# Local attention and a rational-gated MLP in one kernel: one pair of score tiles in other PSUM banks, and the first 259 places of the list of all engines in another order

## The chip, the cores and the metric

The kernel runs on one core of a Trainium2 chip. The metric is device microseconds of one execution, the median of several. A profile of one further execution, with its own time, stands beside the times.

## The reference

Attention over 4 batches, 8 heads, 768 positions, head size 64: each query sees the keys less than 16 positions away, and 24 block keys (the maximum over 32 keys each) whose values are the means of 32 values. Then an MLP with 2048 hidden units over the 3072 tokens of 512 numbers.

```python
k_sum = k.reshape(B, H, nb, 32, D).max(axis=3)
v_sum = v.reshape(B, H, nb, 32, D).mean(axis=3)
scores_l = scale * q @ k.T          # kept where |i - j| < 16
scores_s = scale * q @ k_sum.T + log(32)
a = softmax(concat[scores_l, scores_s])
x = a @ concat[v, v_sum]            # -> (3072, 512)
h = x @ w_in
P = a0 + a1*h + a2*h**2 + a3*h**3
Q = 1 + |b0|*|h| + |b1|*h**2
out = (P / (Q + 1e-06)) @ w_out
```

## The kernel before

The attention is cut into 48 halves of 64 queries (12 to a batch, all 8 heads at once). The MLP is cut into 6 groups of 512 tokens, a group being 8 halves, times 16 chunks of 128 hidden units. Chunk n (n = 0 to 95) is first-layer product, gate and second-layer product; a group's first chunk needs the x of all 8 halves of that group, so no MLP product can start before the first 8 halves are through.

All work is written out by hand as one list, `ORDER` (lines 68 to 113, 1698 places). A wrapper around each engine (`Kept`) makes every instruction follow the engine's last one, so each engine, and SyncE which issues most loads, works strictly in the order of the list. The letters:

- `K0` to `K3` load the keys of the first batch, one pair of heads each, into `kres`; `d0` to `d3` take the block maxima of one pair on VectorE (`ks`). `Q0` loads the queries of halves 0 and 1, `Q1` those of halves 2 to 7. `S`, `I`, `B`, `c`, `F` load or make constants (`F`: the averaging matrix `avg`, kept in `kres`, and values `vf`).
- `b0` to `b3` are the scores of the pairs of halves (0, 1), (3, 6), (4, 2) and (5, 7) on TensorE, into two PSUM tiles `sc` each. `SCP` says from which pool of banks they come: `o` (four banks, later the second layer's output) or `a` (two banks, later squares of h).
- `a0` to `a7` are the nine steps of such a half: peak on VectorE; exponentials on ScalarE; reciprocal on VectorE; multiplication of `ss` on GpSimd (for halves 3 and 5 on VectorE); transposes on TensorE (`pt`); a copy of them (`pts`); values on TensorE (`av`); `xh` on ScalarE or VectorE; `xl` on VectorE. The exponentials read the score tile, so its bank is free when they are done.
- `V` loads the values of a half, `v` (TensorE) and `m` (copies) make the means of the value blocks; `n` and `o` do that for the second batch.
- `W` loads a weight chunk (w_in and w_out, 1 MB, packed; raw tile `wr`, in four buffers in turn, so that W5 takes the buffer of chunk 1 and W8 that of chunk 4), and `w` are the steps that unpack it on ScalarE, GpSimd and VectorE, for some chunks with a DMA issued by GpSimd that writes or adds (`w<-wr`, `wearly<-wr`).
- `A` loads queries and keys of a later half, `L` and `D` do the block maxima of batch 1, `k` copies block keys.
- `h` is a first-layer product (12 matmuls of 512 columns), `g` and `q` are its gate on ScalarE, VectorE and GpSimd (which makes `gl`), `P` is a second-layer product (12 matmuls) that reads `gh` and `gl` of a chunk; it runs three chunks behind `h`.

The buffer of each tile is also written out by hand, in `SLOTS`. Some places have unused matmuls ahead of them (`FILL`), which do no needed work.

Of the kernel before, what the change touches and what calls it, by code (L numbers as in the profile page):

```python
# [76 lines left out]
P11 g9 g9 g10 w12 M g9 g10 w12 q10 h11 a12 a13 b7 a13 g10 q10 P12 a14 V13 a15 h12 g10 a12 a14 g10 g11 w13 a13 a15 q11 w13 g11 q11 g11 w13 a13 W14 g10
g12 a15 w14 g11 P13 a12 g11 g12 a13 a13 g12 g11 q12 h13 w14 a12 P14 V12 a14 a12 a13 g13 w14 a12 w14 g13 a15 V15 q12 w14 w15 a12 g12 a15 A17 w14 a15
a14 h14 g12 a12 g12 g13 q13 q13 a14 V14 a14 a15 w15 g14 g13 w15 w15 a14 g13 w15 w15 P15 h15 a15 a15 g13 P16 q14 L23 q14 a14 g14 g15 A16 a14 q15 g14
h16 L22 g15 b8 q15 g14 g14 a17 g15 g15 g14 g15 g15 g16 h17 g16 P17 q16 P18 q16 g17 A19 g16 a16 g17 q17 A18 f0 g16 f0 g17 q17 h18 g16 D22 g17 h19 g16  # L80
a17 f0 f0 L21 g18 b9 g17 g17 a16 q18 g18 g18 q18 P19 a17 a19 g18 g18 g18 a16 g19 g19 a19 g19 P20 h20 A21 q19 D21 V16 a17 q19 g19 a17 a16 P21 L20 g20
h21 g20 A20 a19 q20 a16 q20 g19 g19 a18 g20 g20 a16 g21 a18 h22 g20 g21 P22 g20 b10 q21 D20 A22 P23 g22 a20 q21 q22 g21 a18 a19 g21 h23 a19 g22 q22
g21 g22 g22 a20 g21 g23 h24 g22 V17 a21 g23 q23 a17 q23 g22 g24 P24 A23 g24 P25 g23 q24 g23 q24 a18 h25 z8 g23 a21 g23 g24 z8 b11 a18 A25 g24 g24 a20
g24 g25 a19 g25 h26 a22 P26 z8 a21 g25 q25 A24 P27 z8 V19 a20 V18 a22 J20 q25 g25 h27 a18 a20 g25 g26 g26 q26 q26 a22 a21 a21 g25 D23 a22 a22 g26 g26
g27 z9 g26 P28 a23 q27 z9 k25 z9 k24 z9 g26 a23 h28 a23 g27 J22 g28 V20 a23 g27 q27 P29 h29 g28 b12 a20 g28 V21 q28 g27 g27 q28 g27 a21 z10 a25 a23
g29 V23 z10 g28 a22 g29 z10 g28 P30 g29 z10 q29 a25 g28 q29 a25 g29 h30 A27 g29 g30 h31 g30 V22 a23 q30 a24 q30 P31 g30 g30 g29 g31 a25 g31 g30 q31
z11 g30 q31 A26 z11 b13 P32 z11 g31 U22 g31 z11 g31 a25 a24 h32 h33 P33 a27 g31 P34 g32 g33 g32 q32 q32 g33 q33 g32 U20 g33 f1 f1 g32 g32 q33 h34 g32
a27 g33 A29 J23 g34 g34 g33 f1 q34 g34 g33 f1 h35 q34 g35 g34 g35 A28 g34 P35 h36 q35 q35 g34 P36 a27 h37 g35 g36 g35 a27 a24 g36 q36 g35 g36 g35 q36
J21 h38 a27 g37 a24 a26 U21 b14 q37 g37 g36 g37 P37 g36 P38 a29 L32 g36 g38 A31 a29 q37 g37 g37 a25 g38 U23 q38 g37 a29 h39 g38 a29 q38 g39 g38 g39
g38 P39 h40 L31 a24 a26 g39 q39 a26 V24 q39 g38 g39 g40 P40 g40 g39 g40 q40 g39 h41 g41 q40 a29 g40 g40 q41 q41 g41 A30 g40 h42 D31 P41 a28 P42 g42  # L90
g41 q42 a26 h43 a24 g42 q42 g41 b15 g42 V25 z12 g41 a31 a28 g42 a27 g41 V27 g43 g42 a26 a30 z12 P43 V26 g43 z12 a28 q43 a31 A32 g43 P44 z12 a28 a30
L33 q43 h44 g42 g44 D32 L30 g43 a31 a28 a26 g43 g43 g44 h45 q44 a31 A33 a30 g44 g45 P45 q44 z13 a31 z13 g44 a30 z13 V28 g45 b16 a32 a32 a28 h46 z13
# [684 lines left out]
```

## Time and profile before

| what | us |
|---|---|
| median of 3 runs | 631.63 |
| lowest and highest | 631.36, 637.08 |
| the profiled execution | 630.29 |
| its span, first to last instruction | 628.4 |
| TensorE busy | 615.1 (98%) |
| VectorE busy | 556.5 (89%) |
| ScalarE busy | 453.4 (72%) |
| GpSimd busy | 251.2 (40%) |

The profiled execution is 1.34 us shorter than the median, and 1.9 us longer than its span. TensorE's share is an average; a busy TensorE may still wait within a group of matmuls or run at the lower clock, so its stages are to be looked at one by one.

### The profile page before, as it was taken

How to read it: one execution, taken by the hardware profiler on the slowest of the kernel's cores; microseconds unless marked ns; L12 is line 12 of the kernel's file. 1: busy time of each engine (PE TensorE's matmuls, PEld its weight loads, DVE VectorE, ACT ScalarE, POOL GpSimd, SP SyncE). 2: the span in 40 equal slices, each digit the busy share in tenths (PEclk: the TensorE clock that was granted, in tenths of full speed). 3: DMA queues.
4: the chain of work that ended last, by engine and by line, in shares of the span. 5: the costliest groups of instructions: out<-in, count | busy, mean ns of one | idle time of the engine just before them, and what ended most of it. 6: DMA issues, size and time to landing. Idle time of an engine off the chain costs nothing.

```text
span 628.4 us, 12096 instructions
## 1 busy us (share of the span) xinstructions
PE 615.1 (98%) x4204; PEld 491.8 (78%) x4204; DVE 556.5 (89%) x1068; ACT 453.4 (72%) x1007; POOL 251.2 (40%) x351
## 2 busy tenths in 40 slices
PE   8899989999999999999999999999999999999997
PEld 4577767778888888878888888888888887878885
DVE  4999999999999898899887999999798897867895
ACT  3998989777968677867785777858777675846553
POOL 0974664771424622334353133354143532221231
PEclk9799999999999999999999999999999999999999
DMA  8998799313342740423353433434413122100001
GB/s 331 340 310 329 221 263 284 118 32 103 121 148 83 213 126 18 159 86 119 111 164 101 143 92 113 145 101 134 136 55 105 59 65 74 68 0 2 0 1 67
DMA packets 52180, 80.78 MB, mean 129 GB/s; under 512 B 6472, under 2 KB 33000, under 8 KB 50200
## 3 DMA queue, kind: packets, MB, share of 16 engines
q1 hardware_dynamic: 50328, 74.87, 36.6%
q0 software_dynamic: 1424, 4.92, 3.5%
q8 instruction: 33, 0.54, 0.4%
q10 hardware_dynamic: 368, 0.22, 0.1%
q14 instruction: 27, 0.22, 0.1%
HBM read 60.33 MB, written 14.75 MB: 119 GB/s over the span
## 4 chain that ended last, share of the span: by engine, by line
PE 79%; DVE 9%; ACT 4%; DMA 3%; POOL 2%; issue 1%; SPq 0%; POOLq 0%; DVEq 0%; ACTq 0%
PE po L162 35%; PE h L162 35%; PE sc L162 4%; PE av L162 4%; DVE tu L162 3%; DVE tq L162 2%; ACT ta L162 2%; DMA w<-wr 1%; PE pt L162 1%; DVE gh L162 1%; DMA kres<-in_kraw_dram 1%; POOL gl L162 1%; DVE wr L162 1%; DMA kr<-in_kraw_dram 1%; DVE sm L162 1%
## 5 line engine op out<-in xcount | busy, mean ns | idle before, releaser
L162 POOL TENSOR_TENSOR gl<-tu,ta 128x512 fp32r<-128x512 f32 x95 | 129.0, 1359 | 325.5 <-DVE tu L162 235.0
L162 PE MATMUL po<-w,gh 128*128 128x512 f32 x384 | 119.9, 394 | 0.0
L162 PE MATMUL po<-wearly,gh 128*128 128x512 f32 x384 | 119.6, 393 | 0.0
L162 PE MATMUL h<-xh,w 128*128 128x512 f32 x384 | 97.8, 393 | 1.7 <-DMA w<-wr 1.5
L162 PE MATMUL h<-xh,wearly 128*128 128x512 f32 x384 | 97.0, 392 | 0.6 <-ACT xh L162 0.6
L162 POOL TENSOR_SCALAR ss<-ss,sm 128x120 f32<-128x120 f32 x184 | 85.8, 487 | 17.1 <-DVE sm L162 9.2
L162 ACT ACTIVATE ta<-tq,cs 128x512 f32<-128x512 f32 x96 | 69.3, 722 | 31.8 <-DVE tq L162 30.2
L162 DVE SCALAR_TENSOR_TENSOR gh<-tu,cs,ta 128x512 fp32r<-128x512 f32 x96 | 77.1, 805 | 11.4 <-ACT ta L162 7.3
L162 PEld LDWEIGHTS h<-xh,w 128*128 128x128 f32 x384 | 71.0, 188 | 18.8 <-DMA w<-wr 2.0
L162 PEld LDWEIGHTS h<-xh,wearly 128*128 128x128 f32 x384 | 71.3, 188 | 16.8 <-ACT xh L162 0.7
L162 ACT ACTIVATE ta<-h,cs 128x512 f32<-128x512 f32 x95 | 64.7, 681 | 26.1 <-POOL gl L162 25.6
L162 PEld LDWEIGHTS po<-wearly,gh 128*128 128x128 f32 x384 | 71.2, 188 | 15.7 <-issue 1.1
L162 PEld LDWEIGHTS po<-w,gh 128*128 128x128 f32 x384 | 71.0, 188 | 15.0 <-issue 0.3
L162 ACT ACTIVATE sq<-h 128x512 f32<-128x512 f32 x72 | 42.0, 583 | 52.5 <-PE h L162 31.6
L162 DVE SCALAR_TENSOR_TENSOR tu<-tu,cs,tq 128x512 f32<-128x512 f32 x96 | 74.9, 780 | 3.4
L162 PE MATMUL po<-wearly,gl 128*128 128x512 f32 x192 | 75.1, 391 | 1.2 <-POOL gl L162 1.2
L162 PE MATMUL po<-w,gl 128*128 128x512 f32 x192 | 75.1, 391 | 0.0
L162 ACT ACTIVATE tu<-h,cs 128x512 f32<-128x512 f32 x96 | 74.5, 776 | 0.0
L162 DVE SCALAR_TENSOR_TENSOR tu<-tu,cs,h 128x512 f32<-128x512 f32 x96 | 71.0, 742 | 1.5
L162 DVE TENSOR_TENSOR tu<-tu,h 128x512 f32<-128x512 f32 x96 | 65.1, 678 | 7.8 <-ACT tu L162 6.6
L162 DVE SCALAR_TENSOR_TENSOR tq<-tq,gh 128x512 f32<-128x512 f32 x96 | 68.6, 714 | 1.8
L162 DVE SCALAR_TENSOR_TENSOR tq<-sq,cs,ta 128x512 f32<-128x512 f32 x72 | 53.4, 743 | 13.7 <-ACT ta L162 13.6
(105 smaller groups left out, 914.1 us busy)
## 6 DMA issues: line engine op xcount, KB each, us to landing
...
cross<-tb SPq DMA_DIRECT2D x32, 256.0 KB
...
out_dram<-o SPq DMA_DIRECT2D x23, 256.0 KB
...
```

Source lines behind the costliest of these rows:

```text
L162: out = getattr(self.engine, name)(*args, **kw)
```

## The change

The first 259 places of `ORDER` hold the same 259 entries in another order; places 260 to 1698 are as before. The third letter of `SCP` becomes `a`, so the score tiles of halves 4 and 2 (`b2`) lie in the two `a` banks. The four score products come as b0, b2, b1, b3 where they came as b0, b2, b3, b1. `SLOTS` is written anew: with it, halves 3 and 6 (`b1`) get the two `o` banks that no tile had before them, and halves 5 and 7 (`b3`) still get those of halves 0 and 1; of all tiles first used after place 259 only two copies (`pts10`, `pts11`) take over from another tile than before, up to a renaming of buffers.

```diff
-SCP = 'ooooaaaa'
+SCP = 'ooaoaaaa'
...
 ORDER = """
-K1 Q0 K0 K3 S K2 W0 w0 d3 d0 w0 d1 d2 b0 a1 a0 Q1 a1 w0 W1 a1 a0 w0 a1 w1 B I b2 a4 b3 a0 a2 a4 W2 w1 a0 a2 w0 a7 F w1 c a4 V7 V4 a1 V3 b1 a2 w2 V6 w0
-w1 a5 V5 a1 w2 w1 a2 a4 V0 w2 a7 w1 a0 v4 v5 v6 a7 k9 a5 v0 a6 V2 a7 v3 V1 A9 v8 v2 A8 a6 w2 v7 a0 v1 v9 m0 a3 a2 W3 a3 a0 w2 a5 a5 W5 m4 a4 m2 a6 m5
-a2 k8 m3 a6 a0 b4 W4 a0 a4 a3 m1 a5 a5 a3 a9 w3 a1 a3 a1 a8 a5 a6 a3 a3 a7 a8 m6 a1 a6 w3 a7 G a2 w3 V8 a5 a2 a3 a8 w5 a4 a6 m7 w2 a7 a6 a6 a5 a2 a4
-w5 a3 a7 w3 w4 a9 w3 a7 a4 a8 h0 V9 w5 g0 w4 w4 L11 h1 w3 a9 w5 n4 n3 g0 W6 q0 g0 w4 q0 W7 g1 w5 n0 w5 g0 A10 n1 a9 a8 a9 a8 a9 g1 g1 g0 q1 q1 g0 g1
-g1 A11 h2 g2 W9 a9 g2 w4 q2 w4 W8 n2 n5 o P3 a9 g2 w6 q2 g1 a9 g2 h3 w6 g3 D11 a8 w6 w7 g2 w7 w6 g3 a8 g2 w6 w9 h4 P4 L10 q3 a8 w7 V11 g4 b5 P5 q3 a10
-q4 g4 g3 g3 g3 w8 w6 h5 q4 w9 a11 w7 g4 w8 h6 g3 A12 a10 g5 P6 w8 g4 g4 g5 q5 w9 w8 g4 w7 w7 L13 W10 a11 q5 a11 P7 g5 w10 D10 w8 g5 V10 a10 h7 w10 g5
...
+K1 K3 d3 d1 K0 S K2 d0 d2 Q0 W0 Q1 b0 b2 w0 a1 a0 b1 a1 a0 w0 w0 W1 a1 V3 V0 a0 w0 b3 w0 a1 k8 a2 w1 w1 a2 a4 k9 I a4 a6 a2 W2 w1 B a6 w2 V2 a0 a2 F
+v3 a4 c a0 V5 V4 V1 a2 V7 v0 a5 V6 v9 a5 a7 a0 w2 a1 v4 v5 v7 a6 w0 v2 a4 w2 a5 w1 a7 v8 a1 v6 a3 v1 w1 m0 a6 w2 a2 A8 m6 a5 w2 w1 a3 A9 a4 m5 W3 W4
+W5 a4 a6 a0 b4 a7 a5 a6 m1 G V8 m2 a5 a6 a0 m4 a3 a8 a3 a7 a6 m7 m3 a2 a3 a2 a3 a1 w3 w3 a6 a5 a0 a9 a2 a7 a8 a3 a7 a3 a5 a4 w3 a4 a5 a8 a1 a7 a4 a3
+a1 a7 w4 w3 a7 w4 h0 w5 w2 h1 w4 a9 n3 w5 n4 w3 n0 w3 w5 a9 a8 n2 g0 n5 w5 n1 g0 W7 W6 q0 q0 V9 g0 w4 w5 w5 a8 a8 g1 h2 w4 a9 g0 g0 L11 g1 a9 o a9 q1
+g0 g1 a8 q1 g1 g2 P3 g1 h3 w4 w6 A10 w7 q2 w6 g2 g2 q2 w7 w6 D11 w6 a9 a8 W9 g2 A11 g2 h4 a8 a9 g1 g3 V11 w6 g2 a9 w6 P4 b5 q3 g3 g4 w7 P5 q3 W8 w9 g3
+q4 a10 h5 g4 L10 g3 g3 q4 w8 w9 a11 w7 g4 w8 h6 g3 A12 a10 g5 P6 w8 g4 g4 g5 q5 w9 w8 g4 w7 w7 L13 W10 a11 q5 a11 P7 g5 w10 D10 w8 g5 V10 a10 h7 w10
...
```

Place 260 is the `w9` of `w9 a11 w7 g4` in the sixth line of either text.

## Rows read from the trace of the kernel before

**Rows 1.** Busy us by stage: length, PE, PEld, DVE, ACT, POOL, clock, DMA share, GB/s.

```profile
5.30:18.95 13.65, 11.16 (x216) 6.41 (x216) 9.98 (x20) 6.82 (x21) 4.29 (x8) 1.00 1.02 398
18.95:25.77 6.82, 5.67 (x73) 3.51 (x73) 6.58 (x14) 6.73 (x28) 6.47 (x8) 0.50 1.07 280
25.77:40.06 14.29, 13.68 (x276) 10.64 (x274) 13.57 (x33) 13.03 (x48) 13.35 (x23) 1.00 1.04 379
40.06:71.55 31.49, 31.07 (x230) 23.88 (x231) 31.07 (x46) 28.99 (x52) 15.98 (x18) 1.00 0.84 271
```

**Rows 2.** TensorE in order of time, 40 to 112 us: start, duration, [idle].

```profile
40.06 2.14 PE L162 MATMUL h<-xh,wearly 128*128 128x512 f32 x8 [0.60 <-ACT xh L162]
...
53.05 0.50 PE L162 MATMUL po<-wearly,gl 128*128 128x512 f32 x1 [0.42 <-POOL gl L162]
...
90.73 1.19 PE L162 MATMUL h<-xh,w 128*128 128x512 f32 x4 [1.55 <-DMA w<-wr]
```

**Rows 3.** GpSimd in order of time, 60 to 92 us.

```profile
75.71 1.29 POOL L162 TENSOR_TENSOR gl<-tu,ta 128x512 fp32r<-128x512 f32 x1 [1.46 <-DVE tu L162]
...
81.38 0.87 POOL L162 DMA_DIRECT2D w<-wr  x1
```

**Rows 4.** Weight loads of TensorE in order of time, 10 to 14 us.

```profile
10.64 0.21 PEld L162 LDWEIGHTS sc<-ks,qres 64*64 64x64 f32 x8 [0.44 <-DVE ks L162]
...
11.49 0.21 PEld L162 LDWEIGHTS sc<-ks,qres 64*64 64x64 f32 x8 [0.53 <-DVE ks L162]
...
13.32 0.21 PEld L162 LDWEIGHTS sc<-kres,qres 64*64 64x64 f32 x8 [0.58 <-DMA qres<-in_qfirst_dram]
```

**Rows 5.** VectorE in order of time, 0 to 36 us.

```profile
7.91 3.53 DVE L162 TENSOR_REDUCE ks<-kres 128x24 f32<-128x768 f32 x4 [6.50 <-DMA kres<-in_kraw_dram]
12.18 0.67 DVE L162 TENSOR_REDUCE sc<-sc 128x4 f32<-128x480 f32 x1 [0.74 <-PE sc L162]
...
20.39 0.28 DVE L162 TENSOR_TENSOR cs<-cs 128x1 f32<-128x1 f32 x1
...
20.89 0.98 DVE L162 TENSOR_TENSOR cs<-cs 128x1 f32<-128x1 f32 x1
...
25.10 1.22 DVE L162 TENSOR_TENSOR wearly<-wr,wearly 128x1024 fp32r<-128x1024 f32 x1
```

**Rows 6.** DMA issues by tile: KB of each.

```profile
kres<-in_kraw_dram SPq DMA_DIRECT2D x4, 400.0 KB
...
qres<-in_qfirst_dram SPq DMA_DIRECT2D x1, 256.0 KB
```

**Rows 7.** ScalarE in order of time, 10 to 46 us.

```profile
11.42 1.16 ACT L162 ACTIVATE wr<-wr 128x1024 f32<-128x1024 f32 x1 [9.39 <-DMA wr<-in_wio_dram]
13.14 0.36 ACT L162 ACTIVATE ss<-sc,sm 128x120 f32<-128x120 f32 x1 [0.56 <-DVE sm L162]
```

**Rows 8.** TensorE in order of time, 8 to 24 us.

```profile
9.71 0.40 PE L162 MATMUL sc<-kres,qres 64*64 64x96 f32 x8
...
15.09 0.40 PE L162 MATMUL sc<-kres,qres 64*64 64x96 f32 x8
...
19.05 0.56 PE L162 MATMUL sc<-bias,hot 96*128 96x480 bf16 x1 [1.66 <-ACT ss L162]
20.66 0.56 PE L162 MATMUL sc<-bias,hot 96*128 96x480 bf16 x1 [1.05 <-ACT ss L162]
21.15 0.60 PE L162 MATMUL sc<-kres,qres 64*64 64x96 f32 x8
```

**Rows 9.** Busy time by stage, columns as in the first group.

```profile
12.18:71.41 59.23, 55.15 (x715) 41.32 (x713) 57.53 (x106) 54.67 (x146) 39.25 (x54) 0.94 0.94 313
...
45.60:71.41 25.81, 25.39 (x208) 19.43 (x206) 25.39 (x38) 23.34 (x38) 13.13 (x13) 1.00 0.85 286
```

**Rows 10.** Busy time of ScalarE alone by stage.

```profile
11.42:43.59 32.17, 30.08 (x105) 0.89 1.04 347
```

**Rows 11.** GpSimd on tile ss, 14 to 48 us: ns least/median/most.

```profile
L162 POOL TENSOR_SCALAR ss<-ss,sm x32: 362/368/2434, 15.6 to 47.2; 128x120 f32<-128x120 f32 x32
```

More of the change, by code (lines that the diff above doesn't have):

```diff
@@ L77 @@
[L77 to L92, printed above, removed]
@@ new lines @@
+g10 g12 a15 w14 g11 P13 a12 g11 g12 a13 a13 g12 g11 q12 h13 w14 a12 P14 V12 a14 a12 a13 g13 w14 a12 w14 g13 a15 V15 q12 w14 w15 a12 g12 a15 A17 w14
+a15 a14 h14 g12 a12 g12 g13 q13 q13 a14 V14 a14 a15 w15 g14 g13 w15 w15 a14 g13 w15 w15 P15 h15 a15 a15 g13 P16 q14 L23 q14 a14 g14 g15 A16 a14 q15
+g14 h16 L22 g15 b8 q15 g14 g14 a17 g15 g15 g14 g15 g15 g16 h17 g16 P17 q16 P18 q16 g17 A19 g16 a16 g17 q17 A18 f0 g16 f0 g17 q17 h18 g16 D22 g17 h19
+g16 a17 f0 f0 L21 g18 b9 g17 g17 a16 q18 g18 g18 q18 P19 a17 a19 g18 g18 g18 a16 g19 g19 a19 g19 P20 h20 A21 q19 D21 V16 a17 q19 g19 a17 a16 P21 L20
@@ new lines @@
+g20 h21 g20 A20 a19 q20 a16 q20 g19 g19 a18 g20 g20 a16 g21 a18 h22 g20 g21 P22 g20 b10 q21 D20 A22 P23 g22 a20 q21 q22 g21 a18 a19 g21 h23 a19 g22
+q22 g21 g22 g22 a20 g21 g23 h24 g22 V17 a21 g23 q23 a17 q23 g22 g24 P24 A23 g24 P25 g23 q24 g23 q24 a18 h25 z8 g23 a21 g23 g24 z8 b11 a18 A25 g24 g24
+a20 g24 g25 a19 g25 h26 a22 P26 z8 a21 g25 q25 A24 P27 z8 V19 a20 V18 a22 J20 q25 g25 h27 a18 a20 g25 g26 g26 q26 q26 a22 a21 a21 g25 D23 a22 a22 g26
+g26 g27 z9 g26 P28 a23 q27 z9 k25 z9 k24 z9 g26 a23 h28 a23 g27 J22 g28 V20 a23 g27 q27 P29 h29 g28 b12 a20 g28 V21 q28 g27 g27 q28 g27 a21 z10 a25
@@ new lines @@
+g39 g38 P39 h40 L31 a24 a26 g39 q39 a26 V24 q39 g38 g39 g40 P40 g40 g39 g40 q40 g39 h41 g41 q40 a29 g40 g40 q41 q41 g41 A30 g40 h42 D31 P41 a28 P42
+g42 g41 q42 a26 h43 a24 g42 q42 g41 b15 g42 V25 z12 g41 a31 a28 g42 a27 g41 V27 g43 g42 a26 a30 z12 P43 V26 g43 z12 a28 q43 a31 A32 g43 P44 z12 a28
+a30 L33 q43 h44 g42 g44 D32 L30 g43 a31 a28 a26 g43 g43 g44 h45 q44 a31 A33 a30 g44 g45 P45 q44 z13 a31 z13 g44 a30 z13 V28 g45 b16 a32 a32 a28 h46
+z13 g45 g44 P46 g44 a32 q45 q45 a33 V29 a33 a29 z14 g45 a30 V31 a31 g46 g45 V30 P47 q46 z14 g46 z14 a32 h47 a33 z14 q46 g45 g46 g46 a30 P48 z15 A34
@@ new lines @@
+g57 g57 a37 a39 P58 g56 g58 V34 a37 z16 q57 a34 g58 q57 J33 a37 P59 g57 q58 a39 g57 q58 g58 g57 A41 a39 a38 a35 g57 h59 a36 g58 a38 g59 g58 h60 U31
+g58 g59 q59 g60 P60 a36 a38 a39 A40 P61 q59 g59 a36 g60 U33 z17 a38 g59 b20 V37 A42 z17 g60 q60 h61 g59 g59 q60 z17 P62 V36 g61 z17 a37 g60 g61 g60
+q61 a36 g61 q61 h62 a38 z18 a39 z18 a41 V39 z18 g60 g62 g61 g61 z18 q62 a41 g62 V38 g62 g61 q62 a40 P63 h63 g63 g62 g63 g62 a40 a41 a38 A43 q63 P64
+q63 a39 b21 z19 g63 g62 z19 a43 A44 g63 a41 z19 a40 z19 a40 a41 a43 P65 a40 h64 g64 g63 g64 q64 h65 g64 q64 g63 g64 g65 g64 P66 g65 V40 h66 f3 q65 g65
@@ new lines @@
+f3 g64 q65 a41 V41 f3 g66 g66 a40 g65 g66 q66 q66 h67 g65 g65 f3 g66 g66 a42 P67 g67 g67 h68 g66 q67 g68 P68 a43 g68 g67 q67 q68 a42 A45 P69 h69 g67
+b22 g67 a42 g67 a42 g68 g69 q68 z20 g68 g69 q69 z20 a45 g68 P70 V43 q69 a42 g69 A47 V42 g69 g68 a44 h70 h71 g69 g70 g69 g70 q70 a45 a45 P71 A46 q70
+g70 a43 g70 g70 g71 z20 q71 a42 a44 P72 q71 g71 g71 h72 g70 a43 h73 g72 g71 z20 g71 g71 g72 q72 q72 g73 g73 P73 g72 q73 a44 P74 q73 a43 g73 g73 h74
+z21 b23 z21 g72 a44 g72 a45 g72 V44 a45 z21 h75 P75 a46 a47 g74 a47 g73 g73 g74 q74 a47 g75 q74 a47 g75 g74 q75 h76 q75 g75 g74 V45 g74 a47 g74 a46
@@ L113 @@
+h89 g87 g87 g87 g87 g89 g88 g89 q89 g88 h90 P90 q89 g89 g89 g89 g90 g90 P91 g90 g89 q90 q90 g90 h91 g91 g91 g91 P92 q91 q91 g91 g90 h92 g90 g91 g92
+g92 g92 q92 g91 q92 h93 g93 g92 P93 h94 g92 g93 g92 q93 g93 q93 g93 g93 g94 g94 P94 q94 g94 g93 h95 q94 g95 P95 g94 P96 g95 g94 g95 q95 q95 g94 g95
+g95 g95 P97 P98 f5 f5 f5 f5
 """
```

39 lines of the change are left out of this document (16 added, 23 removed).

## The prediction

> **What bounds the kernel now.** I first read the busy time by stage [rows 1]. The part that the change touches ends at about 71.5 us. From 40.06 us, where the first MLP product starts, TensorE is busy 31.07 of 31.49 us, at full clock; ahead of that it is not (11.16 of 13.65, 5.67 of 6.82 at clock 0.50, 13.68 of 14.29). So from 40 us on TensorE's own work sets the end, and only what delays it counts. Second, TensorE in order of time shows each such delay up to 112 us [rows 2]: 0.60 us ahead of the first product (for xh, all eight halves), 0.42 ahead of a second-layer matmul (for GpSimd's gl; one more like it, at 84 us, is not shown), 1.55 at chunk 8's product, for a DMA that adds to its weights. The reader is to see how few they are: about 3 us in 72.
>
> Third, who stands behind them. GpSimd issued that DMA at 81.38, in an unbroken row of work that began at 75.71 when VectorE's tu came [rows 3]. VectorE is busy 31.07 of 31.49 us in this stage too, and 57.53 of 59.23 from its first score reduction (12.18) to the end of the touched part [rows 1, 9]. So TensorE and VectorE are full side by side: an earlier start of the products only makes the later waits longer, unless VectorE's queue comes earlier as well. What the change is worth is by how much VectorE is earlier at place 260, since the places behind it are the same.
>
> **The change part by part.**
>
> Key loads and block maxima. Before, VectorE's first reduction waited until 7.91 for the third pair's keys, fourth in SyncE's queue; the four reductions ran to 11.44 [rows 5], and b0's matmuls stopped twice for them, 0.44 and 0.53 us [rows 4]. After, K3 is second, with K0 and the first queries behind it: 400 + 256 = 656 KB less ahead of it [rows 6], at the stage's 398 GB/s [rows 1] 1.65 us, so it lands at some 6.3. Reductions at 0.88 us each (3.53 / 4) then start at 6.3, 7.1, 8.0 and 8.9 and end at 9.7, just when b0's matmuls on keys begin (9.71 [rows 8]). Q0, now fifth, still lands ahead of that: the same five loads are in the queue by then. Both stops go: b0 ends 0.97 us earlier, and VectorE's first score reduction starts at 11.2. If the loads land later than that, b0 keeps part of its stops: bounds 0 to 0.97, taken 0.97.
>
> ScalarE's start does not move: it waits for W0 until 11.42 [rows 7], and the bytes ahead of W0 are the same. The exponentials of half 1, which waited 0.56 us at 13.14, now follow W0's step at once.
>
> Banks and the order of the score products. b2 in the `a` banks waits for nobody's exponentials, but for Q1, as before (matmuls at 13.32, after 0.58 us of waiting [rows 4]); it ends in both at some 14.6, ahead of the next pair's matmuls at 15.09 [rows 8]. b1, which stopped for 1.66 and 1.05 us until ScalarE had read sc of b2's halves [rows 8], has untouched banks and follows at 14.6, b3 at some 16.5 to 18.3. That removes 2.71 us of waiting on TensorE and b1's slow speed (0.60 us for eight matmuls at 21.15 against 0.40 at 15.09, both in [rows 8], the clock at 0.50 and 1.00 [rows 1]). But the score tiles were not what TensorE lacked next: pt of half 0 needs GpSimd's ss, and the averaging matrix F, with V3, V0, W2 and V2 put ahead of it in SyncE's queue, lands at about 20.5: by the tiles' sizes some 6.6 MB are ahead of it, at 398 GB/s and from 18.95 on 280 [rows 1]. TensorE's next entry is v3, which needs it. So its idle time moves from 17.4 to 20.7 to 18.3 to 20.5: nearly all of the 2.7 us is lost here, and I count 0 for it. If F lands sooner, it is worth up to the 0.60 us ahead of h0, more not, because of VectorE. The cost on the other side is in the rivals.
>
> Score tiles of b2 in `a` make vs and b4 wait for the exponentials of halves 2 and 4; these end by my walk at 18.4 and 20.0, behind neither F nor the values: 0.
>
> Loads moved. W5 now stands behind w1's last step on VectorE, which goes from 25.10 [rows 5] to some 30, and G and V8 are queued behind W5 on SyncE. W3 and W4 are issued ahead of it and keep the DMA engines busy to about 33, and in this stage their share is 1.04 [rows 1]; so the queue does not run dry, and the cost is 0 (up to 1 us if w1 slips past 34). V9, L11 and A10 stand behind W6, which waits for chunk 2's DMA; their readers come 8 us later: 0.
>
> VectorE's queue. The 259 places hold the same instructions, so its work is the same; only idle time differs. Before it idled 59.23 - 57.53 = 1.70 us, 0.42 of it after 45.60 [rows 9]. Walking the new order with the durations of before, each instruction starting when the one ahead ends and its inputs are there, I find new waits of 0.3 us (half 0's exponentials), 0.3 (half 4's) and 0.5 at the first gate, because ScalarE reaches it at 43.7, as it did before. That leaves VectorE 0.6 us early at the first gate; the balance of idle time (0.97 + 1.28 - 1.1) gives 1.15. I take 0.9. Bounds: a gain of at most 0.97 + 1.70 = 2.67, if it never idles; a loss as large as its new idle time exceeds 2.67.
>
> Sum: xh of the eight halves come by the walk some 1.2 us earlier, so TensorE has the lead; the DMA for chunk 8 and all gl come 0.9 us earlier with VectorE, and TensorE waits a little longer there. Change: -0.9 us.
>
> On GpSimd the 32 multiplications of ss took 368 ns each at the median and 2434 at the most [rows 11], and on VectorE one operation on a single column took 0.98 us where the same kind took 0.28 beside it [rows 5]. The two engines hold each other up, and a new order deals these collisions anew: 0.70 us of VectorE's work is that one instruction, and I let it go either way.
> The Trainium skill (SBUF — State Buffer, section Who interferes with whom) says that a VectorE instruction with two SBUF inputs contends with a GpSimd instruction that reads SBUF; the 0.98 us operation has two, beside GpSimd's unpacking, and so the trace agrees. By that rule it could fall back to 0.28 and the sum would be -1.6 instead of -0.9.
>
> **The rivals.**
>
> ScalarE sets it (0). It is busy 30.08 of 32.17 us from its fixed start at 11.42 to the first gate [rows 10]; if its new waits (for the transposes and values of the last halves, 0.95 and 0.3 in my walk) eat the 2.09 us of idle time, the gates begin as before. For it: the walk reaches the first gate at 43.7 against 43.59. Against it: from the gates on it has room, 28.99 of 31.49 [rows 1]. Time: as before, 631.6.
>
> VectorE hardly idles (larger gain). All of 2.67, with the collision 3.37: 631.63 - 2.67 to 3.37 = 629.0 to 628.3. Against it: each change of engine in the chains of eight halves ends in some wait.
>
> Slower: a second slow stretch. TensorE ran at 1.2 GHz for 6.82 us after its two waits [rows 1, 8]. After the change it idles 18.3 to 20.5 for F, and again ahead of pt of half 2, for GpSimd. If the slow stretch lasts as long again, to 32.6, it meets the transposes and values, where TensorE is busy 13.68 of 14.29 [rows 1]. At 0.60 for 0.40, 6.82 us hold a third less work: 2.3 us late, less the lead of 1.2, so h0 and VectorE's copies are 1.1 us late: 632.7. It decides from where the second stretch costs more than the lead of 1.2 us.
>
> That b1 keeps its wait can be left out: its banks have no earlier tile.
>
> **How the numbers follow.** The profiled execution would take 630.29 - 0.9 = 629.39; the median of the runs is 1.34 above the profiled one, so I forecast 630.7. Chances: the forecast, with its own 630.1 to 631.2, 0.4; ScalarE 0.2; the larger gain 0.2; slower 0.2. The range takes in the largest gain at 628.3 and the slow rival at 632.7, with 0.3 and 0.7 for the runs of before, which already differ: 628.0 to 633.4. One per cent is 6.3 us, about what a measurement of this kernel can tell from no change; all cases lie within it, so 0.95 for that, and the rest for what the walk may have missed.
>
> **What would show it.** In the changed kernel: reductions of keys from about 6.3; no idle time for DVE ks in b0; VectorE's first score reduction at 11.2; b1 without idle time for ACT ss; TensorE idle until about 20.5 ahead of vs; the first product of h at some 38.9; chunk 8's DMA issued at about 80.5, and TensorE's wait for it 1.5 to 2 us. It would be wrong if TensorE met chunk 8 without a wait, if the clock fell again after 26 us, or if VectorE were behind 71.4 us at place 260.

## The result, and the profile after

The changed kernel takes 635.15 us (median of 20 runs, 633.84 to 641.02), before takes 631.5 (20 runs); the ratio is 1.0054, with an interval of 1.0039 to 1.0069. The ratios here and below leave out disturbed runs, which the medians keep. By the ratio the change costs 3.4 us, where I had forecast a gain of 0.9 (630.7); the time is outside my range (628.0 to 633.4). The profiled execution went from 630.29 to 633.84 us and its span from 628.4 to 632.0, so the two traces show the same loss and can be set against each other.

Busy time by stage after the change: length, TensorE, its weight loads, VectorE, ScalarE, GpSimd, clock, DMA share, GB/s.

```profile
11.00:75.48 64.48, 57.73 (x715) 42.72 (x713) 58.08 (x106) 55.26 (x144) 40.58 (x54) 0.89 0.93 297
...
15.30:28.90 13.60, 11.43 (x153) 7.30 (x152) 10.52 (x29) 10.65 (x41) 10.90 (x20) 0.50 1.07 271
```

The first line runs from VectorE's first score reduction to place 260, as the first of [rows 9] did. VectorE is busy 58.08 us where it was 57.53, but the stretch is 64.48 us long where it was 59.23. It begins 1.18 us earlier (11.00 against 12.18) and ends 4.07 us later (75.48 against 71.41). The second line is new: TensorE has 1.2 GHz (0.50) for 13.6 us where it had 6.82 [rows 1]; ahead of it TensorE had idled 1.76 us for the second query load.

VectorE in order of time, after the change:

```profile
5.58 3.53 DVE L162 TENSOR_REDUCE ks<-kres 128x24 f32<-128x768 f32 x4 [4.17 <-DMA kres<-in_kraw_dram]
11.00 0.67 DVE L162 TENSOR_REDUCE sc<-sc 128x4 f32<-128x480 f32 x1 [1.89 <-PE sc L162]
...
19.83 0.18 DVE L162 RECIPROCAL sm<-sm 128x4 f32<-128x4 f32 x1 [0.70 <-ACT sm L162]
...
23.10 0.56 DVE L162 TENSOR_SCALAR cs<-coef 128x6 f32<-128x6 f32 x1 [1.49 <-DMA coef<-in_b_dram]
...
24.31 0.16 DVE L162 TENSOR_TENSOR cs<-cs 128x1 f32<-128x1 f32 x1
...
35.57 0.18 DVE L162 RECIPROCAL sm<-sm 128x4 f32<-128x4 f32 x1 [0.63 <-ACT sm L162]
...
48.01 0.75 DVE L162 SCALAR_TENSOR_TENSOR tq<-tq,cs,ta 128x512 f32<-128x512 f32 x1 [0.26 <-ACT ta L162]
...
55.64 1.62 DVE L162 SCALAR_TENSOR_TENSOR gh<-tu,cs,ta 128x512 fp32r<-128x512 f32 x1
57.30 1.47 DVE L162 SCALAR_TENSOR_TENSOR tq<-tq,gh 128x512 f32<-128x512 f32 x1
```

The key reductions and the first score reduction are as early as the first step of the prediction had them, and earlier. Then VectorE waits, for ScalarE's sums of exponentials and for the coefficients (`B`). Its first gate is at 48.01, 2.42 us behind before's 45.59; the idle time from the first score reduction to there is 5.88 us where it was 1.28. Its own work in that stretch became 1.0 us less (31.13 busy of 37.01, against 32.13 of 33.41). Behind the first gate two instructions of chunk 1 take 1.62 and 1.47 us, which took 0.75 and 0.69 before: the other 1.65 us of the 4.07. The same gate and the same two instructions before:

```profile
45.59 0.71 DVE L162 SCALAR_TENSOR_TENSOR tq<-tq,cs,ta 128x512 f32<-128x512 f32 x1
...
53.02 0.75 DVE L162 SCALAR_TENSOR_TENSOR gh<-tu,cs,ta 128x512 fp32r<-128x512 f32 x1
53.80 0.69 DVE L162 SCALAR_TENSOR_TENSOR tq<-tq,gh 128x512 f32<-128x512 f32 x1
```

ScalarE, after the change:

```profile
11.92 1.14 ACT L162 ACTIVATE wr<-wr 128x1024 f32<-128x1024 f32 x1 [9.90 <-DMA wr<-in_wio_dram]
...
17.03 1.17 ACT L162 ACTIVATE wr<-wr 128x1024 f32<-128x1024 f32 x1 [0.86 <-DMA wr<-in_wio_dram]
...
25.41 0.36 ACT L162 ACTIVATE ss<-sc,sm 128x120 f32<-128x120 f32 x1 [1.40 <-DVE sm L162]
...
27.69 0.58 ACT L162 COPY pts<-pt 120x512 f32<-120x512 f32 x1 [0.56 <-PE pt L162]
...
32.70 1.10 ACT L162 COPY vw<-vs 24x128 f32<-24x128 f32 x4 [1.11 <-PE vs L162]
...
46.82 0.58 ACT L162 ACTIVATE tq<-h 128x512 f32<-128x512 f32 x1
```

ScalarE reaches its first gate at 46.82 where it was 43.59 [rows 10]: 0.50 from a later start and 2.73 from new waits (34.89 us long, 30.07 busy). Each engine's wait names the other or TensorE, so the row to look for is one engine further on. TensorE:

```profile
13.79 0.40 PE L162 MATMUL sc<-kres,qres 64*64 64x96 f32 x8 [1.76 <-DMA qres<-in_qfirst_dram]
...
20.88 0.42 PE L162 MATMUL sc<-kres,qres 64*64 64x96 f32 x2 [1.34 <-issue]
...
24.03 0.65 PE L162 MATMUL vs<-vr,kres 96*32 96x128 f32 x8 [0.83 <-DMA vf<-in_vpad_dram]
24.62 2.18 PE L162 MATMUL pt<-bias,hot 96*128 96x480 bf16 x5
...
42.25 2.11 PE L162 MATMUL h<-xh,wearly 128*128 128x512 f32 x8 [0.56 <-ACT xh L162]
...
62.05 0.69 PE L162 MATMUL av<-pts,vw 120*64 120x64 f32 x16 [1.45 <-issue]
...
93.90 1.20 PE L162 MATMUL h<-xh,w 128*128 128x512 f32 x4 [0.66 <-DMA w<-wr]
```

b1 no longer waits for exponentials, as forecast. But b3, now last, stops in its middle for 1.34 us for nothing that a semaphore shows ("issue"), and the value means `v3` start at 24.03, not 20.5, with the transposes (`pt`) of half 0 behind them. h starts at 42.25 (40.06 before), chunk 8's product at 93.90 (90.73) with a wait of 0.66 us instead of 1.55 [rows 2]: TensorE is now so late itself that it waits less for that DMA.

The profile's chain of work that ended last leads in after through two loads to the value means `v3`, and from there through the transposes behind them (start, duration):

```profile
5.57 12.19 DMA vr<-in_vpad_dram
...
17.78 6.26 DMA vf<-in_vpad_dram
...
24.05 0.64 PE vs L162 x8
```

### The profile page after: what moved, and what is told of

Read it like the earlier page. It is cut to its first block, busy times and chain, and to the rows that moved or that the text cites. A ratio compares the mean times of both kernels' runs of the same rounds, so it can differ in the third digit from the quotient of the medians.

```text
span 632.0 us, 12103 instructions
## 1 busy us (share of the span) xinstructions
PE 617.4 (98%) x4204; PEld 493.5 (78%) x4204; DVE 556.9 (88%) x1068; ACT 453.5 (72%) x1007; POOL 251.0 (40%) x351
## 4 chain that ended last, share of the span: by engine, by line
PE 73%; DMA 9%; DVE 8%; ACT 6%; issue 2%; POOL 1%; SPq 0%; DVEq 0%; POOLq 0%; ACTq 0%
PE po L162 33%; PE h L162 32%; PE av L162 3%; DVE tu L162 3%; PE sc L162 3%; DVE tq L162 2%; DMA w<-wr 2%; ACT ta L162 2%; DMA vr<-in_vpad_dram 2%; DMA wr<-in_wio_dram 1%; PE pt L162 1%; DMA vf<-in_vpad_dram 1%; DMA kw<-in_kwin_dram 1%; DVE gh L162 1%; ACT wr L162 1%
## 5 line engine op out<-in xcount | busy, mean ns | idle before, releaser
L162 PEld LDWEIGHTS h<-xh,wearly 128*128 128x128 f32 x384 | 71.4, 188 | 17.6 <-DVE tu L162 0.8
```

The source lines that it names most:

```text
L162: out = getattr(self.engine, name)(*args, **kw)
```

## The experiments

Each was run in 5 rounds beside the kernel before; ratios are to before on the same chip. "First gate", "h" and "idle" (VectorE from its first score reduction to the first gate) are us of one profiled execution each. Compare by ratio, since before's own median was 631.5 to 632.6 beside them. `SLOTS` is fitted to each list.

| run | median us | ratio, interval | idle | first gate | h |
|---|---|---|---|---|---|
| before | 631.5 | 1 | 1.28 | 45.59 | 40.06 |
| after | 635.15 | 1.0054, 1.0039 to 1.0069 | 5.88 | 48.01 | 42.25 |
| 1 coefficients early | 635.04 | 1.0034, 1.0007 to 1.0061 | 6.20 | 48.14 | 42.38 |
| 2 banks only | 633.11 | 0.9987, 0.9957 to 1.0018 | 1.25 | 46.19 | 40.60 |
| 3 after to h, then before | 634.42 | 1.0018, 0.9989 to 1.0047 | 4.59 | 46.79 | 40.17 |
| 4 before to h, then after | 633.63 | 1.0011, 0.9984 to 1.0037 | 2.11 | 46.06 | 40.28 |
| 5 unused matmuls | 635.31 | 1.0053, 1.0033 to 1.0072 | 4.80 | 47.38 | 41.60 |
| 6 as 4, GpSimd's product first | 632.66 | 1.0017, 0.9997 to 1.0037 | 2.27 | 45.52 | 39.88 |
| 7 before, 82 instructions more | 630.67 | 0.9988, 0.9974 to 1.0003 | 1.07 | 45.64 | 40.11 |
| 8 keys only | 633.28 | 1.0019, 1.0000 to 1.0039 | 3.65 | 47.09 | 41.88 |
| 9 four edits | 636.97 | 1.0078, 1.0060 to 1.0095 | 7.33 | 50.91 | 44.46 |
| 10 the same, product first | 636.31 | 1.0072, 1.0050 to 1.0094 | 7.54 | 49.38 | 43.62 |
| 11 as 9, no unused matmuls | 636.32 | 1.0069, 1.0053 to 1.0084 | 6.38 | 48.62 | 42.86 |
| 12 as 9, chunk 1 as in after | 634.98 | 1.0044, 1.0023 to 1.0065 | 5.91 | 49.45 | 43.68 |
| 13 VectorE fed | 634.93 | 1.0038, 1.0009 to 1.0067 | 5.56 | 48.17 | 42.41 |
| 14 the same, product first | 634.59 | 1.0036, 1.0013 to 1.0058 | 6.58 | 48.43 | 42.69 |
| 15 as 13, no unused matmuls | 635.61 | 1.0042, 1.0018 to 1.0066 | 6.34 | 48.11 | 42.35 |
| 16 as 13 to h, then before | 633.37 | 1.0011, 0.9982 to 1.0041 | 6.76 | 49.06 | 42.43 |
| 17 as 13, transposes first | 635.37 | 1.0046, 1.0028 to 1.0064 | 4.71 | 48.17 | 41.73 |
| 18 as 17 to h, then before | 633.79 | 1.0025, 0.9996 to 1.0053 | 3.86 | 45.96 | 39.34 |

**Parts of the change (runs 1 to 4).** Run 1 moves the coefficients' load:

```diff
-w0 w0 W1 a1 V3 V0
+w0 w0 W1 B a1 V3 V0
...
-W2 w1 B a6 w2
+W2 w1 a6 w2
```

> The changed kernel with one entry moved: the load of the gate's coefficients (B) stands right behind W1, ahead of V3 and V0. Theory A (late loads): VectorE's wait of 1.49 us for coef goes, ScalarE's wait of 1.40 us behind it too, and the kernel is 1.0 to 1.5 us faster than the changed one (633.7 to 634.2 against 635.15). Theory B (the slow clock sets it: TensorE runs at 1.2 GHz for 13.65 us where it ran so for 6.82 us): the transposes and values are as late as before, and the time stays within 0.4 us of 635.15. Theory C (the loss is made behind h0): no change either.

Run 2 is before with the banks alone:

```diff
-SCP = 'ooooaaaa'
+SCP = 'ooaoaaaa'
```

> The kernel before with the change of banks alone: the list is that of before, the score tiles of halves 4 and 2 lie in the two a banks, those of halves 3 and 6 in the o banks that no tile had before. If the change of banks is harmless and the new order alone is at fault (A, B and C alike): b1's 2.71 us of waiting go or turn into waits for something else, and the time is within 1 us of 631.5, more likely 0.3 to 0.6 us below. If the banks are at fault: slower by 1 us or more, with TensorE waiting at vs or b4 for the exponentials of halves 4 and 2.

Run 3 takes the list of after up to and with the first `h0`, and the entries left in the order of before; run 4 is the opposite.

```diff
-w3 a7 w4 h0 w5 w2 h1 w4 a9 n3 w5 n4 w3
+w3 a7 w4 h0 w5 w2 w5 a9 w3 a8 V9 w5 g0
```

> The list of the changed kernel up to and with h0 (158 places), then the rest of the 259 in the order of before. Theories A and B (the loss is made ahead of h0): as slow as the changed kernel, 634.5 to 635.5. Theory C (the loss is made behind h0, above all by TensorE's wait of 1.45 us at av of half 9): 632 to 633.

> The list and banks of the kernel before up to and with h0, then the rest of the 259 places in the order of the changed kernel. Theories A and B: as fast as before, 631 to 632. Theory C: 633 to 635.

The banks alone neither cost nor gain beyond the uncertainty. In run 2's profile b1 no longer waits for exponentials, but stops for "issue" in their place, so b1's wait had hidden that stop (TensorE, run 2):

```profile
20.04 0.40 PE L162 MATMUL sc<-kres,qres 64*64 64x96 f32 x8 [1.67 <-issue]
```

Neither half of the order has the whole loss; the two ratios (0.18 and 0.11%) are each within their own uncertainty. In the profiles each is late mainly in its own half: run 3 is 1.2 us late at the first gate (46.79) and still 1.2 at VectorE's first row from place 260 on, the score reduction that starts at 72.52 (71.33 before); run 4 is 0.5 us late at the first gate and 1.9 at that row (73.21). The table by clock below bears on both halves. Run 1 shows no gain over after (1.0034 and 1.0054, with intervals that overlap): the coefficients are no longer waited for, but VectorE's next entries wait as much:

```profile
22.95 0.67 DVE L162 TENSOR_REDUCE sc<-sc 128x4 f32<-128x480 f32 x1 [1.33 <-PE sc L162]
...
29.92 0.69 DVE L162 COPY pts<-pt 120x512 f32<-120x512 f32 x1 [1.28 <-PE pt L162]
```

The first of these waits for b3 behind its stop (3.42 us in this run), the second for transposes at 1.2 GHz. In after the wait for the coefficients stood ahead of both and covered them.

**Clock, collisions, instructions, keys (runs 5 to 8).**

```diff
-FILL = {'b0': 3, 'b4': 3, 't2': 5, 't0': 5}
+FILL = {'b0': 3, 'b4': 12, 't2': 5, 't0': 5}
```

> The kernel after, with nine more unused matmuls in the place where TensorE waits for the second query load (FILL of b4 12 where it was 3). Clock theory (the kernel after loses because TensorE idles at that wait and its clock then stays at half for 13.7 us where it was 6.8): the half-clock stretch falls back to about 7 us, the first product of h starts at about 41 where it was 42.25, and the time is 633 to 634 us. Order theory (loss by waits and collisions of VectorE, at any clock): the stretch may shrink, but the time stays at 634.5 to 635.5. Code theory (TensorE stops at its 449th instruction for a fetch of 16 KB of instructions): the new matmuls put 18 instructions ahead of that point, so the stop of about 1.7 us, which ended at 20.87 after, is found 18 instructions earlier in the program, and ends at 20 to 21 again.

Run 5: the half-clock stretch is 6.8 us again and b3 does not stop (it ends at 18.66, 23.20 after), which the code theory had not expected. Yet the median is as the order theory had it, as slow as after. In the profile TensorE then waits for what `F` loads, the averaging matrix and values:

```profile
23.09 0.66 PE L162 MATMUL vs<-vr,kres 96*32 96x128 f32 x8 [4.44 <-DMA vf<-in_vpad_dram]
```

Run 6 moves one GpSimd entry behind the first product:

```diff
-g1 g2 P3 g1 h3 w4 w6 A10 w7 q2
+g1 g2 P3 g1 g1 h3 w4 w6 A10 w7 q2
...
-h4 a8 a9 g1 g3 V11
+h4 a8 a9 g3 V11
```

> The kernel before up to the first product of h and the order of after behind it (that ran at 633.6 us, ratio 1.0011), with GpSimd's product of chunk 1 moved ahead of the unpacking of chunks 6 and 7. Collision theory (the loss behind the first product is VectorE's gate of chunk 1, gh 0.75 to 1.40 us and tq 0.69 to 1.47 us, slowed by two GpSimd steps of unpacking issued back to back): gh and tq fall to 0.8 and 0.7 us, TensorE's wait of 1.19 us ahead of the values of half 9 falls under 0.5, place 260 comes at about 71.9 where it was 73.2, and the time is 632.0 to 632.6. Rival (the loss there is a wait for weights or for ScalarE): the two instructions may change, but the time stays at 633.4 or more.

VectorE on chunk 1 in run 4, and then in run 6:

```profile
53.62 1.40 DVE L162 SCALAR_TENSOR_TENSOR gh<-tu,cs,ta 128x512 fp32r<-128x512 f32 x1
55.06 1.47 DVE L162 SCALAR_TENSOR_TENSOR tq<-tq,gh 128x512 f32<-128x512 f32 x1
```

```profile
53.08 0.75 DVE L162 SCALAR_TENSOR_TENSOR gh<-tu,cs,ta 128x512 fp32r<-128x512 f32 x1
53.87 0.69 DVE L162 SCALAR_TENSOR_TENSOR tq<-tq,gh 128x512 f32<-128x512 f32 x1
```

Without GpSimd's two unpacking steps beside them both are back at 0.75 and 0.69, TensorE's wait ahead of the values of half 9 (1.45 us in after, 1.19 in run 4) is gone, and the first row from place 260 on comes at 71.83, as expected. So the collision is shown. Of the 1.38 us that this row is earlier than in run 4, 0.54 lie ahead of the first gate (45.52 against 46.06), which the edit does not touch. Behind the gate VectorE gains 0.84: the two instructions give back 1.43, and the moved unpacking makes it wait later (VectorE, run 6):

```profile
58.91 1.22 DVE L162 SCALAR_TENSOR_TENSOR wr<-wr 128x1024 int32<-128x1024 int32 x1 [0.52 <-POOL wr L162]
```

What this is worth in time the ratios don't tell (1.0011, 1.0017, on different chips); the table by clock below puts it at 1.0 to 1.1 us.

Run 7 puts 82 more TensorE instructions into the warm-up of before:

```diff
-    for i in range(NWARM):
+    for i in range(4):
         pe.matmul(warm, zero[:, 0:P], zero, start=True, stop=True)
+    none = zero[:, 0:64].bitcast(BF16)
+    for i in range(45):
+        pe.matmul(warm[:, 0:P], none, none, start=True, stop=True)
```

> The kernel before with a warm-up of 4 fp32 and 45 small bf16 unused matmuls in place of its own, 82 TensorE instructions more, so that TensorE's 449th instruction falls into the scores of halves 5 and 7. Code theory: those scores stop there until about 20 to 21 us (16.41 us before), the scores of halves 3 and 6 behind them are as late as before or later, VectorE waits some 3 us for halves 5 and 7, and the time is 2 us or more above the kernel before (633.5 to 635.5). Rival (the stop belongs to the banks, or to what the instruction does): the scores of halves 5 and 7 end at 16.4 as before, and the time is within 0.7 us of the kernel before.

```profile
15.73 0.26 PE L162 MATMUL sc<-ks,qres 64*64 64x24 f32 x6
16.65 0.23 PE L162 MATMUL sc<-ks,qres 64*64 64x24 f32 x1 [0.67 <-issue]
```

The stop for "issue" is now in b3, which ran through before; counted over TensorE's records (matmuls, weight loads and semaphore instructions) it stands behind the 449th, as it does after. So the code theory had its place right and its size wrong: TensorE idles 0.67 us for it, where a packet on an instruction queue started 1.5 us ahead of TensorE's reaching that place, and the time is not above before's.

Run 8 is before with the keys' part of the new order:

```diff
-K1 Q0 K0 K3 S K2 W0 w0 d3 d0 w0 d1 d2 b0 a1 a0 Q1
+K1 K3 d3 d1 K0 S K2 d0 d2 Q0 W0 w0 w0 b0 a1 a0 Q1
```

> The kernel before with the key loads, the block maxima and the query load in the order of after, and nothing else. Prediction's first term (0.97 us earlier on VectorE, kept to the end): VectorE's first score reduction at 11.0 to 11.2 where it was 12.18, place 260 at 70.4 to 70.9 where it was 71.33, and the time 0.5 to 1.0 us under the kernel before. Rival (ScalarE, which starts at W0's landing as before, takes the lead away): the reduction comes as early, VectorE idles as much longer ahead of the first gate, and the time is within 0.4 us of the kernel before.

Neither holds: there is no gain, and by the ratio the time is 1.2 us above before, with an interval that ends at none. The reduction comes at 11.90 (the warm-up, slow until the clock rose at 6.9 us in this run, ends at 9.54 and b0 behind it), and half the clock then lasts until 30.7 us over the value means, 0.66 us for eight matmuls where 0.40 is usual:

```profile
28.70 0.66 PE L162 MATMUL vs<-vf,kres 128*32 128x128 f32 x8
```

```profile
32.57 0.69 DVE L162 COPY pts<-pt 120x512 f32<-120x512 f32 x1 [2.51 <-PE pt L162]
```

The second fence is VectorE: its copy of the transposes of half 2 waits 2.51 us, nearly all of its new idle time.

**Taking waits away (runs 9 to 12).** Run 9 has run 5's matmuls and these moves; run 10 adds run 6's; run 11 has 3 unused matmuls again, run 12 the three `w1` where after has them.

```diff
-w0 w0 W1 a1 V3 V0 a0 w0 b3 w0 a1 k8 a2 w1 w1 a2 a4 k9 I a4 a6 a2 W2 w1 B a6 w2 V2 a0 a2 F v3
+w0 w0 W1 B a1 V3 V0 a0 w0 b3 w0 a1 k8 a2 a2 a4 k9 I a4 a6 a2 F W2 a6 w1 w1 w1 w2 V2 a0 a2 v3
```

> The kernel after with four edits ahead of the first product of h: nine more unused matmuls in the wait for the second query load, the coefficients' load right behind the load of chunk 1, the averaging matrix's load ahead of the load of chunk 2, and the unpacking of chunk 1 (all three engines) behind the exponentials of half 6. Theory of waits (the loss ahead of the first product is that VectorE waits 1.49 us for the coefficients, ScalarE 0.86 us for chunk 1 and 1.11 us for the value means, and each makes the other wait): VectorE's idle time from its first score reduction to the first gate falls from 5.87 to under 2.5 us, the first gate comes at 45.0 to 46.2 (48.01 after, 45.59 before), h at 39.5 to 40.8, and the time is 631.5 to 633.0 us. Rival (in this order of entries the two engines wait for each other whatever is loaded when, as the early coefficients alone suggested): the idle time stays above 4 us and the time at 634 to 635 us.

> The kernel of the run before this one in the list, with GpSimd's product of chunk 1 also ahead of the unpacking of chunks 6 and 7. If the loss is the waits ahead of the first product and the collisions of VectorE's chunk 1 behind it, and the two add up: gh at 0.8 and tq at 0.7 us, TensorE's wait for the values of half 9 under 0.5 us, place 260 at 70.8 to 71.9, 1.0 to 1.5 us under the run with the waits alone, that is 630.3 to 632.0 us, at or under the kernel before. If the collisions cost nothing that is not given back later: within 0.5 us of the run with the waits alone.

> The three edits of loads and unpacking without the unused matmuls. Clock theory: TensorE idles 1.8 us for the second query load, its clock falls to half for 10 us or more, the transposes and values are late, and the time is 0.7 to 1.5 us above the same kernel with the unused matmuls. Rival (the clock ahead of the first product is hidden behind VectorE and ScalarE): a longer half-clock stretch, but within 0.4 us of it.

> The unused matmuls and the two loads earlier, with the unpacking of chunk 1 where after has it. If ScalarE's wait for chunk 1 counts by itself: ScalarE waits 0.8 to 0.9 us at about 17, VectorE 0.7 and 0.3 us for the sums of halves 2 and 4, first gate 0.8 to 1.3 us later than with the unpacking moved, and the time 0.8 to 1.3 us above it. If it is hidden: within 0.4 us.

My theory of single waits falls here, and by my own edits: all four are as slow as after or slower. VectorE's part of `w1` follows ScalarE's, which I had put behind three halves of exponentials (run 9, VectorE):

```profile
23.09 1.23 DVE L162 SCALAR_TENSOR_TENSOR wr<-wr 128x1024 int32<-128x1024 int32 x1 [4.12 <-DMA wr<-in_wio_dram]
```

The trace names the DMA, but ScalarE's step on the same tile ended at 23.00. And `F` brings values as well as the matrix: in run 12, where it stands ahead of W2, ScalarE waits 2.29 us for W2, for which it does not wait in after. The DMA engines are full there (share 1.05 from 15 to 29 us), so a load moved up is paid by the one behind it.

**TensorE's own order (runs 13 to 18).** Run 13 moves no large load; it has run 5's matmuls and

```diff
-w0 w0 W1 a1 V3 V0
+w0 w0 W1 B a1 V3 V0
...
-I a4 a6 a2 W2 w1 B a6 w2
+I a4 a6 W2 w1 w0 a2 a6 w2
...
-a1 v4 v5 v7 a6 w0 v2
+a1 v4 v5 v7 a6 v2
```

Run 14 adds run 6's move, run 15 has 3 unused matmuls, run 16 the order of before behind the first `h0`.

> The kernel after with VectorE kept fed, and no large load moved: the 3 KB of coefficients right behind chunk 1's load, nine more unused matmuls in the wait for the second query load (which also put TensorE's stop for instructions elsewhere), and on VectorE the last unpacking of chunk 0 and the unpacking of chunk 1 ahead of the reciprocal of half 2. Theory of VectorE's waits (0.70 for half 2's sums, 1.49 for the coefficients and what stands behind them): its idle time ahead of the first gate falls from 5.87 to 2.5 to 3.5 us, the first gate comes at 45.2 to 46.4, h at 39.7 to 41, and the time is 632 to 633.3 us. Rival (the order loses by its mix: ScalarE waits for chunk 1, the value means and VectorE, whatever VectorE does): idle time over 4.3 us, first gate at 47 or later, 634 to 635.5 us.

> The run before this one in the list with GpSimd's product of chunk 1 ahead of the unpacking of chunks 6 and 7. Collisions behind the first product add: 0.8 to 1.3 us under the run without it, TensorE's wait for the values of half 9 gone. If they are given back at the later waits: within 0.5 us.

> The first run of this list without the nine unused matmuls: TensorE idles 1.8 us at the query load and stops at its 449th instruction, in the scores of halves 5 and 7, until 20 to 21 us. If the clock and the stop count once VectorE is fed: first gate 0.7 to 1.5 us later, and the time as much above the run with the matmuls. If they are hidden: within 0.4 us.

> The first run of this list up to the first product of h, and the order of before behind it. If the front then costs nothing against before (first gate at 45.2 to 46.2): 630.8 to 632.2 us, within 0.7 us of the kernel before, and a point lower if the earlier start is kept. If the front still loses: as the run with after's front (ratio 1.0018) or above, 632.5 to 634 us.

Run 14's move does in the profile what it did in run 6: from the first gate to the first row from place 260 on VectorE takes 26.39 us where run 13 took 27.40 (26.48 against 27.40 in runs 10 and 9, 26.31 against 27.15 in runs 6 and 4). By the ratios neither this nor the unused matmuls (runs 11 and 15) makes a difference clear of the uncertainty.

For run 13 the rival's numbers came: idle 5.56, first gate 48.17. But now the rows show one entry that holds the others (run 13, TensorE, then VectorE and ScalarE):

```profile
24.37 0.65 PE L162 MATMUL vs<-vr,kres 96*32 96x128 f32 x8 [5.27 <-DVE sm L162]
24.96 2.18 PE L162 MATMUL pt<-bias,hot 96*128 96x480 bf16 x5
```

```profile
29.99 0.69 DVE L162 COPY pts<-pt 120x512 f32<-120x512 f32 x1 [1.44 <-PE pt L162]
```

```profile
28.03 0.58 ACT L162 COPY pts<-pt 120x512 f32<-120x512 f32 x1 [1.62 <-PE pt L162]
```

`v3` stands at the head of TensorE's queue for 5.27 us (the engine named had long been done; SyncE issued the averaging matrix at 17.84 only), and the transposes behind it, whose input was ready, make both engines wait. In after and in runs 1, 3, 5, 13 and 15 the chain of work that ended last passes through `v3`, which starts there between 22.55 and 24.44 us, and the transposes behind it. Runs 17 and 18 move it:

```diff
-F v3 a4 c a0 V5 V4 V1 a2 V7 v0
+F a4 c a0 V5 V4 V1 a2 V7 v3 v0
```

> The kernel with VectorE kept fed (635 us, VectorE's first gate at 48.18), with one entry moved: the value means of half 3 (v3), which wait for the averaging matrix until 24.4 us at the head of TensorE's queue, stand behind the transposes of halves 0 and 2 and no longer ahead of them. Theory of the averaging matrix (v3 holds back the transposes of halves 0 and 2, these VectorE's copy for 1.44 us and ScalarE's for 1.62 us, and the means behind them ScalarE's copy for 1.12 us): TensorE's wait of 5.27 us is under 2, the copies wait under 0.3 us, VectorE's idle time ahead of the first gate falls from 5.56 to under 3 us, the first gate comes at 45.2 to 46.4, h at 39.7 to 40.8, and the time falls by 1.5 to 2.5 us to 632.5 to 633.5. Rival (the idle time only moves, as in the runs before): idle time over 4.3 us, first gate at 47 or later, time within 0.8 us of 635.

> The same front, and the order of before behind the first product of h. If the front is then as good as that of before: first gate at 45.2 to 46.4, place 260 at 71 to 72, 630.5 to 632.2 us, within 0.7 us of the kernel before or under it. If the front still loses: first gate at 48 or later and 633 to 634 us, as the same with v3 ahead of the transposes (633.4).

By their medians, neither expectation of a gain holds. By the profiles there are two cases. In run 18's, TensorE has half the clock for 3.4 us, and the front is level with that of before: h at 39.34, first gate at 45.96 (40.06 and 45.59 before), span 628.2 (busy time by stage, then TensorE):

```profile
22.20:25.60 3.40, 3.40 (x18) 1.84 (x22) 3.02 (x11) 3.37 (x16) 3.23 (x6) 0.50 1.07 264
```

```profile
18.62 1.19 PE L162 MATMUL pt<-bias,hot 96*128 96x480 bf16 x5
...
25.22 0.60 PE L162 MATMUL vs<-vr,kres 96*32 96x128 f32 x8
...
39.34 1.89 PE L162 MATMUL h<-xh,wearly 128*128 128x512 f32 x7 [0.56 <-ACT xh L162]
```

In run 17's, the same front has half the clock for 6.8 us, from 26.8, over values and transposes, and VectorE's copy waits 1.31 us (busy time by stage, then VectorE):

```profile
26.80:33.60 6.80, 6.22 (x80) 4.82 (x80) 5.26 (x9) 4.81 (x24) 4.20 (x7) 0.50 1.06 372
```

```profile
31.90 0.69 DVE L162 COPY pts<-pt 120x512 f32<-120x512 f32 x1 [1.31 <-PE pt L162]
```

Each run comes with its mean granted clock, so the medians can be split by it. In the 20 profiles a mean of 0.996 goes with 3.4 us of half clock in all after the first rise (the last few us of the span left out), 0.993 to 0.995 with 6.8, 0.990 to 0.992 with 10.2 and 0.989 with 13.6. The number of runs is in brackets; before are the 133 runs taken beside the experiments; means under 0.990 are left out:

| run | 0.996 and over | 0.993 to 0.995 | 0.990 to 0.992 |
|---|---|---|---|
| before | 631.36 (38) | 631.51 (53) | 633.08 (33) |
| after | none of 20 | 634.75 (6) | 635.69 (8) |
| 3 after to h, then before | none | 633.20 (4) | 636.29 (2) |
| 4 before to h, then after | 633.63 (5) | 633.83 (7) | none |
| 6 as 4, GpSimd's product first | 632.51 (3) | 632.84 (8) | 632.18 (1) |
| 7 before, 82 instructions more | 630.10 (3) | 630.59 (5) | 630.84 (3) |
| 13 VectorE fed | 633.82 (3) | 635.28 (8) | 638.17 (1) |
| 16 v3 first, then before | 632.45 (7) | 634.45 (5) | none |
| 18 transposes first, then before | 630.93 (5) | 633.86 (4) | 636.36 (1) |

At the highest clock, moving `v3` is worth 1.5 us (run 18 against 16), and run 18 stands level with before or 0.4 us under it; one step lower the gain is 0.6 and both are 2 to 3 us above before, while before loses 0.15. The groups are small, the two ran on different chips, and the fastest run of 16 (631.07) lies within those of 18 (630.08 to 631.49), so this supports the reading and does not settle it.

The same table answers a question that the ratios leave open. At the same clock after is 3.2 and 2.6 us above before, and its six runs under 0.990 have 635.49, 0.7 more than those at 0.993 to 0.995. So the longer slow stretch is a small part of its loss. Run 4 is 2.3 us above before in both columns, run 6 1.1 and 1.3: the order behind the first product does cost, and moving GpSimd's product takes back about half. Run 3 is 1.7 us above before at 0.993 to 0.995, with 4 runs only. The split was made after the times were known.

## Why the prediction was wrong

**What bounds it:** right. From the first product on TensorE and VectorE are full side by side, the value of the change is VectorE's time at place 260, and that is where it stands: 4.07 us late there, 3.6 at the end. It is also the sign of being wrong that came: place 260 at 75.48, behind 71.4.

**Key loads:** right by the profile (5.58 where I had 6.3, first reduction at 11.00 where I had 11.2; 1.18 us against 0.97). By its own durations the walk's four reductions end at 9.8, not 9.7, which changes little. As a gain it is not shown: the keys alone (run 8) brought none.

**ScalarE's start:** 11.92 where I held it fixed at 11.42, a miss of 0.5.

**Banks and b1:** right that b1's waiting is no loss to be won back (run 2). Wrong in the sizes behind it: I had b3 end at 18.3 and `v3` start at 20.5; they were at 23.20 and 24.03. b3's stop was hidden under b1's wait before, as run 2 shows (1.67 us). The averaging matrix was the mis-sized term: I worked out when the bytes ahead of it would have moved, but SyncE issued it only at 17.02 (8.92 before). That it then shared full engines with the loads issued behind it is my reading, not shown by a run. SyncE's rows of after:

```profile
11.91 0.33 SPq L162 DMA_DIRECT2D coef<-in_b_dram  x1
13.77 0.33 SPq L162 DMA_DIRECT2D vr<-in_vpad_dram  x1
17.02 0.33 SPq L162 DMA_DIRECT2D kres<-in_cavg_dram  x1
```

**VectorE's queue:** the step that failed. My walk had 1.1 us of new waits; idle time grew by 4.6 us to 5.88 ahead of the first gate. It took the coefficients as landed (1.49 us) and ScalarE as late as before (it is 3.2 us later), and it ended each wait where the next began, with no price for an instruction behind the waiting one. Which single wait was first is not settled: runs 1, 5, 9 to 13 each removed one or more, and the idle time went to another row. What after and the runs 1, 5 and 13 share is `v3` on the chain that ended last. Of the fronts in after's order only that with `v3` moved has its first gate back at 45.96 in a profile (run 18), and there the half clock was short as well.

**Collisions:** "I let it go either way" was the right doubt and the wrong count. The 0.98 us operation [rows 5] became 0.16, and gh and tq, each with two inputs beside GpSimd's unpacking, became 1.62 and 1.47, back at 0.75 and 0.69 in run 6. In the traces of after and of run 4 each of the slowed gh and tq ends 0.52 to 0.55 us after the GpSimd instruction beside it, and before's operations of 0.28 and 0.98 us end within 0.01 us of GpSimd's: VectorE is held until GpSimd is done. So the 0.28 us that the prediction took as free was itself held. The Trainium skill (SBUF — State Buffer, section Who interferes with whom) has the rule that the prediction quotes; the traces agree. The prediction drew the gain of 0.70 us from it; the loss of 1.65 us at chunk 1 was to be had from the same rows, by walking GpSimd's order behind the first product as well.

**Rivals:** ScalarE is as late as VectorE, not on time. The slow rival had the right sign and 0.2, but not the cause: in the profile there is not a second stretch of 1.2 GHz but one of 13.6 us in place of 6.82, and by the last table the longer stretch is worth 0.7 us of after's loss. The prediction put before's stretch after two waits; it began at 18.95, ahead of the second. Before is little hurt by 6.8 us of it (631.51 against 631.36), and more by 10.2 (633.08). Fronts that put transposes and values there lose 1.5 to 3 us at 6.8 (runs 13, 16 and 18). That before is spared because its half clock fell on b1's waiting (18.95 to 25.77 in [rows 1]) is argued, not shown.

**What a measurement can tell:** the prediction took one per cent as about the limit. 20 runs of each kernel told 0.54% with an interval of 0.39 to 0.69.

No run beats both kernels by its ratio beyond the uncertainty; the nearest is run 7 (0.9988). At the same clock it lies 0.9 to 2.2 us under before; why is not known.
